# An inverse Fourier transform's last step: rows of four positions packed into three sets of matmul weights, with shared partial products added in PSUM

## The chip, the core and the metric

The kernel runs on one NeuronCore of one Trainium2 chip. The metric is the device time of one execution in microseconds (us); it was 1055.1 us (median of 3 runs, 1054.97 to 1055.27) before the change.

## The reference

Two batches of 3008 positions with 256 channels, all in float32, pass through a convolution by Fourier transform along the positions and then two feed-forward layers. Cut to what matters:

```python
X = np.fft.rfft(x, axis=1)                       # x: (2, 3008, 256)
Y = X * (filt_r + 1j * filt_i)[None]
y = np.fft.irfft(Y, n=3008, axis=1)
h = y.reshape(6016, 256) @ w_in                  # 256 -> 2048
g = np.where(h > 0, h, np.exp(np.minimum(h, 0)) - 1)
z = g @ w_out                                    # 2048 -> 256
h2 = z @ w2_in
out = (h2 * np.clip(h2 + 3, 0, 6) / 6) @ w2_out
```

## The kernel before, in words

The transform of length 3008 = 47 x 64 is done as two small transforms, each a matmul with a constant matrix: 47 points (`s1`, `s1t` forward, `i1` back) and 64 points (`s2` forward, `i2` back). The work is cut by batch b (0, 1) and by half h of the channels (128 channels each). The way back is: the product with the filter (`mult`, on DVE, with a sum on POOL), `i2_mm` on PE, `i2_evac` (a copy out of PSUM on ACT), a store to a scratch array in DRAM (`scr2`, 96 rows, line 233), a reload in another order (`v_load`, line 237), and `i1_mm`, the last step, whose results `i1_evac` copies into blocks of 512 positions (`yblk`). Those blocks are split into a high and a low part (`x_split`) for the matmuls of the feed-forward layers.

In `i1_mm` the reloaded data are the stationary operand (the weights, 96 rows by 128 channels for one of 32 places j) and the constant matrix `i1` (96 x 94) is streamed, so one j gives 94 positions. Five j share a PSUM bank and make a group, so a half has seven groups, the last one of two. The profile counts each float32 matmul of this kind as two PE records, and each has a weight load of its own.

Batch 0 is worked off ahead of the feed-forward layers, in an order written out by hand, the string `PROLOGUE`. A letter is a step, and the digits behind it are the half and the number: `S` the forward matmul and the filter, `I` the inverse of 64 points with its store, `V` the reload of a half, `O` or `o` one group of the last step (with its copy on ACT or on DVE), `X` the split of a block, `b` and `B` the first step of batch 1, `G` and `H` the first units of the feed-forward layer, `c` and `k` pieces of the preparation of weights, `F` the sign of a filter on POOL. So O00 is the first group of half 0, I15 the last inverse of half 1. Every engine works through its own instructions in the order in which the program issues them.

Batch 1 is put into the stream of the feed-forward units by slots (`pre` and `post`): a function `i1` places the reloads four slots ahead of a group, the group behind a unit, and the copy one slot later. Transfers of the rotated tiles go out on SP's queue in the program's order. Pools: `p4` has 21 tiles of 4 KB per partition, `p2` 20 of 2 KB, `ps` 7 banks of PSUM, `const` holds the matrices.

Of the kernel before, what the change touches and what calls it, by code (L numbers as in the profile page):

```python
# [9 lines left out]
F32 = mybir.dt.float32  # L10
# [9 lines left out]
NB, NA = 47, 64  # L20
NK2 = NB // 2 + 1
NJ = NA // 2
DFF = 2048
P = 128
NF = DFF // P
TJ = 2 * NB
TG = 5
KP = 96
# [19 lines left out]
def fft_conv_moe_moe2(ctx, tc, xp, fq, sg, cs1, cs1t, cs2, ci2, ci1, ident, w1i, w1o, w2i, w2o, out):  # L48
    nc = tc.nc
    const = ctx.enter_context(tc.tile_pool(name="const", bufs=1))  # L50
# [10 lines left out]
    def name(s):  # L61
        uid[0] += 1
        return f"{s}_{uid[0]}"

    def t4(shape, dt=F32):
        return p4.tile(shape, dt, tag="t4", name=name("t4"))

    def t2(shape, dt=F32):
        return p2.tile(shape, dt, tag="t2", name=name("t2"))

    def bank():
        return ps.tile([P, 512], F32, tag="ps", name=name("ps"))
# [4 lines left out]
    def evac(eng, dst, src):  # L77
        if eng is nc.scalar:
            nc.scalar.activation(dst, src, AF.Copy)
        else:  # L80
            eng.tensor_copy(dst, src)
# [10 lines left out]
    def flat(t):  # L92
        return t.rearrange("p k d -> p (k d)")
# [17 lines left out]
    mats = {}  # L111

    def load_mat(key, src, queue=nc.scalar):
        k, m = src.shape
        mats[key] = const.tile([k, m], F32, name=key)
        queue.dma_start(mats[key], src)
# [11 lines left out]
    scr2 = [[dram.tile([KP, NJ * P], F32, name=f"scr2_{b}_{h}") for h in range(2)] for b in range(B)]  # L128
# [5 lines left out]
    xin, filt, zs, ws, vin, accs, yblk = {}, {}, {}, {}, {}, {}, {}  # L134

    def x_load(b, h, q):
        xin[b, h, q] = t4([P, 8, P])
        nc.sync.dma_start(xin[b, h, q][:KP], xp[b, h, :, 8 * q : 8 * q + 8, :])
# [93 lines left out]
            nc.scalar.activation(flat(o), acc, AF.Copy)  # L232
        nc.sync.dma_start(by_a(scr2[b][h], g), o)

    def v_load(b, h, q):
        vin[b, h, q] = t4([KP, 8, P])
        nc.sync.dma_start(flat(vin[b, h, q]), scr2[b][h][:, 8 * q * P : 8 * (q + 1) * P])

    EDGES = [sum(BLOCKS[:i]) for i in range(len(BLOCKS) + 1)]
    JG = -(-NJ // TG)  # L240

    def i1_mm(b, h, jg):
        accs[h, jg] = bank()
        for j in range(jg * TG, min(NJ, jg * TG + TG)):
            nc.tensor.matmul(  # L245
                accs[h, jg][:, (j - jg * TG) * TJ : (j - jg * TG + 1) * TJ],
                vin[b, h, j // 8][:, j % 8, :], mats["i1"], start=True, stop=True,
            )

    def i1_evac(b, h, jg, eng):  # L250
        acc = accs.pop((h, jg))
        lo, hi = jg * TG * TJ, min(NJ, jg * TG + TG) * TJ
        for bl in range(len(BLOCKS)):
            a, e = max(lo, EDGES[bl]), min(hi, EDGES[bl + 1])
            if a < e:
                if (b, bl) not in yblk:
                    yblk[b, bl] = t4([P, 2, 512])
                evac(eng, yblk[b, bl][:, h, a - EDGES[bl] : e - EDGES[bl]], acc[:, a - lo : e - lo])
# [562 lines left out]
    pre = [[] for _ in range(NS)]  # L821
    post = [[] for _ in range(NU + 8)]

    def at(slots, n, fn, *args):
        slots[n].append(lambda: fn(*args))
# [12 lines left out]
    def fetch1(f):  # L838
# [12 lines left out]
        T00 T01 T02 S00 T03 F01 S01 T04 F01 S02 T05 F01 S03 I00 F01 S04 I01 F01 A10 A11 F01  # L851
        S05 I02 A12 A13 A14 I03 F01 A15 A16 I04 T10 c01 T11 c01 w00 I05 F01 x00 x01 V00 T12
        S10 T13 S11 T14 F01 S12 T15 S13 I10 F01 S14 I11 S15 I12 O00 I13 b00 c01 O01 I14 c01
        b01 o02 I15 M00 c01 b02 V10 c01 O03 X00 O04 w01 b03 c01 X01 k02 O05 O06 X02 k02 B00
        B01 B02 B03 G00 G01 k03 O10 o11 G02 X10 o12 X11 O13 X12 o14 k02 H00 H01 k02 O15 k01
        H02 O16
    """
    LOADS = [(0, None, q, None) for q in range(4)]
    for x in "F00 F01 F02 F03 X0 X1 X2 X3 F04 F05 F10 W0 M F11 F12 F13 F14 F15".split():
# [89 lines left out]
    for i, (l, p) in enumerate(ROUNDS):  # L949
        start = NU + 4 * GROUPS * (i - 1)  # L950
# [34 lines left out]
        at(pre, t + 4, i2_evac, 1, h, g)  # L985

    def i1(h, jg, t):
        for q in range(4):
            if (8 * q // TG) == jg:
                at(pre, t - 4, v_load, 1, h, q)  # L990
        at(post, t, i1_mm, 1, h, jg)
        at(pre, t + 1, i1_evac, 1, h, jg, nc.scalar)

    T = NI * NF
# [7 lines left out]
        mid(0, g, T + 12 + 2 * g)  # L1002
    for g in range(6):
        mid(1, g, T + 24 + 2 * g)
    for jg in range(7):
        i1(0, jg, T + 32 + jg)
    for jg in range(7):
        i1(1, jg, T + 42 + max(0, jg - 1))

    with tc.manual_schedule():  # L1010
        load_mat("s1t", cs1t, nc.sync)
        for key, src in (("id", ident), ("sg", sg), ("s2", cs2), ("i2", ci2), ("i1", ci1)):
            load_mat(key, src)
        three = const.tile([P, 1], F32, name="three")
        nc.vector.memset(three, 3.0)
        engs = (nc.scalar, nc.vector)

        warm = const.tile([P, 512], F32, name="warm")
        nc.gpsimd.memset(warm, 0.0)
        acc = bank()  # L1020
        for n in WARM:
            nc.tensor.matmul(acc[:, :n], warm[:, :P], warm[:, :n], start=True, stop=True)
        for h, g, q, r in LOADS:
            if q is not None:
                x_load(0, h, q)
            elif g is not None:
                f_load(0, h, g)
            elif r is not None:
                w_raw(0, r)
            else:  # L1030
                load_mat("s1", cs1, nc.sync)
        for jg in range(JG):
            s1t(0, 0, jg, engs[jg % 2])
        lead = w_chain(0, WLEAD, lambda f: None)
        f_sign(0, 0, 0)
        f_sign(0, 0, 1)
        nsign = 2
        for step in PROLOGUE.split():
            what, h, g = step[:-2], int(step[-2]), int(step[-1])
            if what == "T":  # L1040
                tr(0, h, g, nc.scalar if g > 1 else engs[g])
            elif what == "S":
                s2_mm(0, h, g)
                mult(0, h, g)
            elif what == "A":
                s1t(0, h, g, engs[g % 2])
            elif what == "I":
                i2_mm(0, h, g)
                i2_evac(0, h, g)
            elif what == "V":  # L1050
                for q in range(4):
                    v_load(0, h, q)
            elif what == "O":
                i1_mm(0, h, g)
                i1_evac(0, h, g, nc.scalar)
            elif what == "o":
                i1_mm(0, h, g)
                i1_evac(0, h, g, nc.vector)
            elif what == "k":
                steps(conv, g)  # L1060
            elif what == "c":
                steps(lead, g)
            elif what == "X":
                x_split(0, g, h)
            elif what == "F":
                for _ in range(g):
                    f_sign(0, *divmod(nsign, 6))
                    nsign += 1
            elif what == "x":
                x_load(1, h, g)  # L1070
            elif what == "w":
                w_raw(0, WLEAD + g)
            elif what == "b":
                s1_split(h, g)
            elif what == "B":
                s1_mm(1, h, g, parts.pop(("x", h, g)))
                s1_evac(1, h, g)
            elif what == "G":
                g1_half(units[g], 0)
            elif what == "H":  # L1080
                g1(units[g])
                if g:
                    g_split(units[g - 1])
            elif what == "M":
                split_mat("s1")

        for n, u in enumerate(units):
            place[0] = n
            for fn in pre[n]:
                fn()  # L1090
            if n >= NI:
                g1(u)
                g_split(units[n - 1])
            if n >= SKEW:
                g2(units[n - SKEW])
            for fn in post[n]:
                fn()
# [113 lines left out]
```

## Time and profile before

| What | Value |
|---|---|
| median of 3 runs | 1055.1 us |
| profiled execution, its own time | 1063.18 us |
| its span, first to last instruction | 1061.4 us |
| PE busy | 1048.8 us, 99% |
| DVE, ACT, POOL busy | 886.1, 797.7, 202.7 us |
| line 245 on PE (`i1_mm`) | 256 records |

The span is the profiled execution's first to last instruction; 1.8 us of its time lie around it. The profiled execution is 8.1 us longer than the median of the runs, so its durations make a sum against 1063.2 us, and the difference is carried over to the median. PE is TensorE's matmuls and PEld its weight loads, which the profile counts apart. DVE, ACT, POOL and SP are the vector, scalar, GpSimd and sync engines. [...]

### The profile page before, as it was taken

How to read it: one execution, taken by the hardware profiler on the slowest of the kernel's cores; microseconds unless marked ns; L12 is line 12 of the kernel's file. 1: busy time of each engine (PE TensorE's matmuls, PEld its weight loads, DVE VectorE, ACT ScalarE, POOL GpSimd, SP SyncE). 2: the span in 40 equal slices, each digit the busy share in tenths (PEclk: the TensorE clock that was granted, in tenths of full speed). 3: DMA queues.
4: the chain of work that ended last, by engine and by line, in shares of the span. 5: the costliest groups of instructions: out<-in, count | busy, mean ns of one | idle time of the engine just before them, and what ended most of it. 6: DMA issues, size and time to landing. Idle time of an engine off the chain costs nothing.

```text
span 1061.4 us, 14383 instructions
## 1 busy us (share of the span) xinstructions
PE 1048.8 (99%) x5022; PEld 918.7 (87%) x5022; DVE 886.1 (83%) x1427; ACT 797.7 (75%) x1437; POOL 202.7 (19%) x218
## 2 busy tenths in 40 slices
PE   9999999999999999999999999999999999999998
PEld 7688888888889989988888888888888888888998
DVE  2899999898886799889989978888888888888776
ACT  2478888897767888877877867777777777777766
POOL 1720000444546745300021100010010010000000
PEclk9999999999999999999999999999999999999999
DMA  9785100374645454610365710100100100100100
GB/s 278 246 263 198 50 16 1 106 222 151 196 135 178 153 193 152 213 55 6 133 236 161 231 73 21 60 1 21 60 14 27 40 18 18 41 1 1 40 1 35
DMA packets 57944, 107.31 MB, mean 101 GB/s; under 512 B 5008, under 2 KB 33680, under 8 KB 57872
## 3 DMA queue, kind: packets, MB, share of 16 engines
q1 hardware_dynamic: 52144, 88.21, 25.3%
q0 software_dynamic: 4896, 17.83, 5.4%
q8 instruction: 39, 0.64, 0.3%
q10 hardware_dynamic: 832, 0.36, 0.1%
q14 instruction: 33, 0.27, 0.1%
HBM read 69.42 MB, written 36.96 MB: 100 GB/s over the span
## 4 chain that ended last, share of the span: by engine, by line
PE 82%; ACT 7%; DVE 7%; issue 2%; DMA 2%; POOL 1%; SPq 0%; DVEq 0%; ACTq 0%; POOLq 0%
PE ps L90 24%; PE ps L88 24%; PE ps L89 24%; PE ps L158 2%; PE lone L88 1%; PE lone L90 1%; PE lone L89 1%; PE ps L245 1%; DVE t L85 1%; ACT t L84 1%; DMA scr<-t 1%; POOL t L217 1%; DVE t L679 1%; PE ps L202 1%; DVE t L634 1%
## 5 line engine op out<-in xcount | busy, mean ns | idle before, releaser
L88 PE MATMUL ps<-t,w 128*128 128x512 f32 (+1 forms) x1120 | 421.2, 376 | 2.3 <-DVE t L634 1.3
L90 PE MATMUL ps<-t,w 128*128 128x512 f32 (+1 forms) x1120 | 420.2, 375 | 0.7 <-DVE t L85 0.6
L89 PE MATMUL ps<-t,w 128*128 128x512 f32 (+1 forms) x1120 | 419.6, 375 | 0.2 <-DVE w L316 0.2
L88 PEld LDWEIGHTS ps<-t,w 128*128 128x128 f32 x1120 | 211.7, 189 | 29.4 <-DVE t L498 1.9
L90 PEld LDWEIGHTS ps<-t,w 128*128 128x128 f32 x1120 | 211.6, 189 | 28.4 <-DVE t L679 2.2
L89 PEld LDWEIGHTS ps<-t,w 128*128 128x128 f32 x1120 | 211.7, 189 | 25.9 <-DVE w L316 1.6
L679 DVE TENSOR_TENSOR t<-t,t 128x512 fp32r<-128x512 f32 (+1 forms) x256 | 175.7, 701 | 24.1 <-ACT t L674 22.5
L674 ACT ACTIVATE t<-t 128x512 fp32r<-128x512 f32 (+1 forms) x256 | 154.0, 616 | 6.1 <-DVE t L664 5.7
L628 ACT ACTIVATE t<-ps 128x512 f32<-128x512 f32 (+1 forms) x176 | 103.2, 586 | 64.9 <-PE ps L90 63.3
L634 DVE TENSOR_TENSOR t<-ps,t 128x512 f32<-128x512 f32 (+1 forms) x176 | 118.1, 679 | 14.2 <-ACT t L628 13.0
L664 DVE SCALAR_TENSOR_TENSOR t<-t,t 128x512 f32<-128x512 f32 (+1 forms) x144 | 97.6, 705 | 33.3 <-ACT t L648 32.7
L648 ACT ACTIVATE t<-t,three 128x512 f32<-128x512 f32 (+1 forms) x144 | 97.2, 707 | 37.3 <-DVE t L634 36.6
L495 ACT ACTIVATE t<-ps 128x512 f32<-128x512 f32 (+1 forms) x128 | 74.1, 579 | 30.1 <-PE ps L90 28.1
L84 ACT ACTIVATE t<-t 128x512 fp32r<-128x512 f32 (+2 forms) x108 | 66.2, 618 | 22.5 <-POOL t L217 20.0
L496 ACT ACTIVATE t<-t 128x512 f32<-128x512 f32 (+1 forms) x128 | 79.3, 619 | 4.1
L85 DVE TENSOR_TENSOR t<-t,t 128x512 fp32r<-128x512 f32 (+2 forms) x96 | 73.3, 769 | 10.6 <-ACT t L84 10.4
L548 POOL TENSOR_TENSOR t<-t,t 128x512 f32<-128x512 f32 (+1 forms) x12 | 16.2, 1351 | 286.0 <-DVE t L634 257.0
L498 DVE SCALAR_TENSOR_TENSOR ps<-t,ps 128x512 f32<-128x512 f32 (+1 forms) x76 | 50.4, 663 | 23.0 <-ACT t L496 22.5
L88 PE MATMUL ps<-t,t 128*128 128x512 f32 (+1 forms) x160 | 60.2, 376 | 0.6 <-DVE t L634 0.6
L89 PE MATMUL ps<-t,t 128*128 128x512 f32 (+1 forms) x160 | 60.1, 376 | 0.0
L90 PE MATMUL ps<-t,t 128*128 128x512 f32 (+1 forms) x160 | 60.1, 376 | 0.0
L85 DVE TENSOR_TENSOR t<-ps,t 128x512 fp32r<-128x512 f32 (+1 forms) x76 | 49.9, 656 | 0.1
(115 smaller groups left out, 1520.6 us busy)
## 6 DMA issues: line engine op xcount, KB each, us to landing
t<-in_fq SPq DMA_DIRECT2D x24, 512.0 KB, 6.2
scrw<-t SPq DMA_DIRECT2D x16, 512.0 KB, 2.8
w<-scrw POOLq DMA_DIRECT2D x16, 512.0 KB, 5.0
t<-in_xp SPq DMA_DIRECT2D x16, 384.0 KB, 6.0
scr<-t SPq DMA_DIRECT2D x24, 256.0 KB, 3.0
t<-scr SPq DMA_DIRECT2D x16, 384.0 KB, 5.2
scrx<-t SPq DMA_DIRECT2D x10, 512.0 KB, 3.3
t<-scr POOLq DMA_DIRECT2D x10, 512.0 KB, 6.1
```

Source lines behind the costliest of these rows:

```text
L84: nc.scalar.activation(hi, src, AF.Copy)
L85: eng.tensor_tensor(out=lo, in0=src, in1=_f32(hi), op=ALU.subtract)
L88: nc.tensor.matmul(acc, wh, xh, start=start, stop=False, skip_group_check=more)
L89: nc.tensor.matmul(acc, wl, xh, start=False, stop=False, skip_group_check=more)
L90: nc.tensor.matmul(acc, wh, xl, start=False, stop=stop, skip_group_check=more)
L496: nc.scalar.activation(t[:, :n], t[:, :n], AF.Exp, scale=-1.0)
L628: nc.scalar.activation(like(t, self.n), got(bank_, self.n), AF.Copy)
L634: nc.vector.tensor_tensor(out=like(self.h[key], n), in0=got(bank_, n), in1=like(u, n), op=ALU.add)
L648: nc.scalar.activation(like(r, n), h, AF.Relu, bias=three)
L664: stt(out=r, in0=r, scalar=6.0, in1=h, op0=ALU.min, op1=ALU.mult)
L674: nc.scalar.activation(gh[:, : self.n], g[:, : self.n], AF.Copy)
L679: nc.vector.tensor_tensor(out=gl[:, :n], in0=g[:, :n], in1=_f32(gh[:, :n]), op=ALU.subtract)
```

## The change

Of the 96 rows of a place j, the last step now needs three kinds of weights for four places. Rows of an even place fill partitions 0 to 95 of a tile, and 32 rows of the odd place beside it fill partitions 96 to 127 (tiles 0 and 1, eight such pairs each). The 64 rows that are left of two odd places fill a third tile, shared by all groups of the half. A group is four places (376 positions): two matmuls of 141 columns, which give the even place and one part of the odd one, and one matmul of 2 x 94 columns with weights from the shared tile, which adds the rest of both odd places in PSUM. A half has eight groups of three matmuls instead of seven with 32 in all. The matrix `i1` becomes two padded ones (`i1a`, 141 columns, `i1b`, 188), zeroed and loaded in six pieces on POOL's queue at the start. The reload of a half becomes eight transfers into three tiles instead of four into four, in runs of 512 bytes. `PROLOGUE` gets O07 and O17, and X12 moves behind o14. In batch 1 all eight transfers of a half go out four slots ahead of its first group. The warm-up's tile moves from `const` to `p2`.

```diff
-    def v_load(b, h, q):
-        vin[b, h, q] = t4([KP, 8, P])
-        nc.sync.dma_start(flat(vin[b, h, q]), scr2[b][h][:, 8 * q * P : 8 * (q + 1) * P])
+    def v_load(b, h):
+        by_j = scr2[b][h].rearrange("r (j d) -> r j d", d=P)
+        for i in range(2):
+            t = vin[b, h, i] = t4([P, 8, P])
+            nc.sync.dma_start(t[:KP], by_j[:, 16 * i : 16 * i + 16 : 2])
+            nc.sync.dma_start(t[KP:], by_j[0:64:2, 16 * i + 1 : 16 * i + 16 : 2])
+        t = vin[b, h, 2] = t4([P, 8, P])
+        for i in range(2):
+            nc.sync.dma_start(t[64 * i : 64 * i + 16], by_j[64:KP:2, 2 * i + 1 : NJ : 4])
+            nc.sync.dma_start(t[64 * i + 16 : 64 * i + 64], by_j[1:KP:2, 2 * i + 1 : NJ : 4])
+
+    def load_i1():
+        for key, n in (("i1a", TJ + NB), ("i1b", 2 * TJ)):
+            mats[key] = const.tile([P, n], F32, name=key)
+            nc.gpsimd.memset(mats[key], 0.0)
+        one, both = mats["i1a"], mats["i1b"]
+        nc.gpsimd.dma_start(one[:KP, :TJ], ci1)
+        nc.gpsimd.dma_start(one[KP:, TJ:], ci1[0:64:2, :NB])
+        for i in range(2):
+            r, c = 64 * i, TJ * i
+            nc.gpsimd.dma_start(both[r : r + 16, c : c + NB], ci1[64:KP:2, :NB])
+            nc.gpsimd.dma_start(both[r + 16 : r + 64, c + NB : c + TJ], ci1[1:KP:2, NB:])
...
     def i1_mm(b, h, jg):
-        accs[h, jg] = bank()
-        for j in range(jg * TG, min(NJ, jg * TG + TG)):
+        acc = accs[h, jg] = bank()
+        for i in range(2):
+            n = 2 * jg + i
             nc.tensor.matmul(
-                accs[h, jg][:, (j - jg * TG) * TJ : (j - jg * TG + 1) * TJ],
-                vin[b, h, j // 8][:, j % 8, :], mats["i1"], start=True, stop=True,
+                acc[:, 2 * TJ * i : 2 * TJ * i + TJ + NB], vin[b, h, n // 8][:, n % 8, :], mats["i1a"],
+                start=i == 0, stop=False, skip_group_check=True,
             )
+        nc.tensor.matmul(
+            acc[:, : IG * TJ].rearrange("p (a b) -> p a b", a=2)[:, :, TJ:], vin[b, h, 2][:, jg, :],
+            mats["i1b"].rearrange("p (a b) -> p a b", a=2), start=False, stop=True, skip_group_check=True,
+        )
...
     def i1(h, jg, t):
-        for q in range(4):
-            if (8 * q // TG) == jg:
-                at(pre, t - 4, v_load, 1, h, q)
+        if jg == 0:
+            at(pre, t - 4, v_load, 1, h)
...
-    for jg in range(7):
-        i1(1, jg, T + 42 + max(0, jg - 1))
+    for jg in range(8):
+        i1(1, jg, T + 42 + min(5, max(0, jg - 1)))
```

What this does to the engines' own orders shows at three places. The first is PE in batch 0, from the inverse I11 (its matmul is the first row) to the last inverse I15. Line 202 is the forward matmul of 64 points, line 222 the inverse, line 245 the last step; `t_97` and `t_98` are the first two reloaded tiles, `i_117` is `i1`. Before:

```order
L222 MATMUL ps_531<-t_118_484,i_115 128x512
L245 MATMUL ps_536<-i_117,t_97_429 128x94 x5
L222 MATMUL ps_544<-t_124_500,i_115 128x512
L245 MATMUL ps_554<-i_117,t_97_429 128x94 x3
L245 MATMUL ps_554<-i_117,t_98_431 128x94 x2
L222 MATMUL ps_563<-t_130_515,i_115 128x512
L245 MATMUL ps_573<-i_117,t_98_431 128x94 x5
L222 MATMUL ps_582<-t_136_529,i_115 128x512
L245 MATMUL ps_607<-i_117,t_98_431 128x94
```

After the change the last step is lines 266 and 270; `t_98`, `t_99` are the tiles of pairs, and `t_100` is the shared one:

```order
L222 MATMUL ps_542<-t_118_495,i_115 128x512
L266 MATMUL ps_547<-i1a,t_98_437 128x141 x2
L270 MATMUL ps_547<-i1b,t_100_443 128x2x94
L222 MATMUL ps_553<-t_124_511,i_115 128x512
L266 MATMUL ps_563<-i1a,t_98_437 128x141 x2
L270 MATMUL ps_563<-i1b,t_100_443 128x2x94
L222 MATMUL ps_570<-t_130_526,i_115 128x512
L266 MATMUL ps_580<-i1a,t_98_437 128x141 x2
L270 MATMUL ps_580<-i1b,t_100_443 128x2x94
L222 MATMUL ps_587<-t_136_540,i_115 128x512
```

Between two inverses a group of five matmuls has become one of two and one, and the first group reads the shared tile already.

The second place is SP's queue, from the last store of half 1 of batch 0 over the reload of that half to the raw weights behind it. Before:

```order
L233 DMA scr_0_1_83<-t_148_565 128x4x128
L233 DMA scr_0_1_83<-t_154_584 128x4x128
L237 DMA t_157_596<-scr_0_1_83 96x1024
L237 DMA t_158_598<-scr_0_1_83 96x1024
L237 DMA t_159_600<-scr_0_1_83 96x1024
L237 DMA t_160_602<-scr_0_1_83 96x1024
L267 DMA raw_629<-in_w1i 128x2x256
```

After the change:

```order
L233 DMA scr_0_1_83<-t_148_572 128x4x128
L233 DMA scr_0_1_83<-t_154_589 128x4x128
L239 DMA t_157_601<-scr_0_1_83 96x8x128
L240 DMA t_157_601<-scr_0_1_83 32x8x128
L239 DMA t_158_604<-scr_0_1_83 96x8x128
L240 DMA t_158_604<-scr_0_1_83 32x8x128
L243 DMA t_159_607<-scr_0_1_83 16x8x128
L244 DMA t_159_607<-scr_0_1_83 48x8x128
L243 DMA t_159_607<-scr_0_1_83 16x8x128
L244 DMA t_159_607<-scr_0_1_83 48x8x128
L292 DMA raw_631<-in_w1i 128x2x256
```

The four transfers of 96 rows have become eight of 96, 32, 16 and 48 rows at the same place between the last store and the raw weights, and those of the shared tile come last.

The third place is PE where half 1 of batch 0 begins its last step, behind a unit's three matmuls (lines 88 to 90, weights `w`). `t_157` and `t_158` are reloaded tiles. Before:

```order
L88 MATMUL ps_697<-t_171_637,w_604 128x512
L89 MATMUL ps_697<-t_171_637,w_604 128x512
L90 MATMUL ps_697<-t_172_638,w_604 128x512
L245 MATMUL ps_706<-i_117,t_157_596 128x94 x5
L245 MATMUL ps_713<-i_117,t_157_596 128x94 x3
L245 MATMUL ps_713<-i_117,t_158_598 128x94 x2
L88 MATMUL ps_721<-t_180_663,w_604 128x512
L89 MATMUL ps_721<-t_180_663,w_604 128x512
```

After the change, where `t_157` holds pairs and `t_159` is the shared tile:

```order
L88 MATMUL ps_705<-t_169_639,w_612 128x512
L89 MATMUL ps_705<-t_169_639,w_612 128x512
L90 MATMUL ps_705<-t_170_640,w_612 128x512
L266 MATMUL ps_714<-i1a,t_157_601 128x141 x2
L270 MATMUL ps_714<-i1b,t_159_607 128x2x94
L266 MATMUL ps_719<-i1a,t_157_601 128x141 x2
L270 MATMUL ps_719<-i1b,t_159_607 128x2x94
L88 MATMUL ps_725<-t_179_666,w_612 128x512
```

The place of the groups in PE's order is the same; the first one again reads the tile that is reloaded last.

## Rows read from the trace of the kernel before

**Rows 1.** The page, parts 1 and 4: busy us (share) xinstructions, and the chain.
```profile
PE 1048.8 (99%) x5022; PEld 918.7 (87%) x5022; DVE 886.1 (83%) x1427; ACT 797.7 (75%) x1437; POOL 202.7 (19%) x218
...
PE 82%; ACT 7%; DVE 7%; issue 2%; DMA 2%; POOL 1%; SPq 0%; DVEq 0%; ACTq 0%; POOLq 0%
```

**Rows 2.** Line 245 by shape: xcount, busy us, mean ns, idle before.
```profile
L245 PE MATMUL ps<-i,t 96*128 96x94 f32 x256 | 31.6, 273 | 0.0
```

**Rows 3.** Timeline of the weight loads: start us, us, engine, line, xcount.
```profile
54.39 1.09 PEld L245 LDWEIGHTS ps<-i,t 96*128 96x128 f32 x9 [0.24 <-issue]
```

**Rows 4.** Timeline of PE, 44 to 62 us, columns as above.
```profile
44.38 1.02 PE L202 MATMUL ps<-t,s 128*128 128x512 f32 x2
...
45.24 0.60 PE L171 MATMUL ps<-id,zt 128*128 128x128 f32 x4
...
54.39 1.25 PE L245 MATMUL ps<-i,t 96*128 96x94 f32 x10
...
60.27 1.13 PE L222 MATMUL ps<-t,i 128*128 128x512 f32 x2 [0.42 <-POOL t L217]
```

**Rows 5.** Line 237's first two sets of reloads: issues, then us to landing.
```profile
L237 SPq DMA_DIRECT2D t<-scr x4: 311/370/377, 48.3 to 49.7; - x4
...
DMA to landing us min/median/max: 5.5/7.1/8.2
...
L237 SPq DMA_DIRECT2D t<-scr x4: 321/370/411, 64.5 to 65.8; - x4
...
DMA to landing us min/median/max: 3.9/5.5/7.0
```

**Rows 6.** Timeline of PE, 64 to 79 us.
```profile
64.95 0.44 PE L88 MATMUL ps<-t,s_h 96*96 96x512 f32 x1
...
68.89 2.37 PE L245 MATMUL ps<-i,t 96*128 96x94 f32 x20
...
75.04 0.46 PE L88 MATMUL ps<-t,w 128*128 128x512 f32 x1
...
78.55 0.46 PE L88 MATMUL ps<-t,w 128*128 128x512 f32 x1
```

**Rows 7.** Windows: busy us of each engine, granted clock, DMA share, GB/s.
```profile
57.50:59.50 2.00, 1.99 (x13) 1.39 (x12) 1.99 (x4) 1.49 (x5) 0.96 (x2) 1.00 1.13 340
...
67.00:71.00 4.00, 4.00 (x30) 3.70 (x28) 3.83 (x8) 3.68 (x8) 0.00 (x0) 1.00 1.03 262
```

**Rows 8.** Timeline of PE at 87 us.
```profile
87.53 0.48 PE L88 MATMUL ps<-t,w 128*128 128x512 f32 x1 [0.76 <-DVE t L498]
```

**Rows 9.** Timeline of PE, batch 1.
```profile
305.36 1.35 PE L245 MATMUL ps<-i,t 96*128 96x94 f32 x10
...
314.31 1.25 PE L245 MATMUL ps<-i,t 96*128 96x94 f32 x10
...
315.35 0.44 PE L88 MATMUL ps<-t,w 128*128 128x448 f32 x1
...
339.71 2.37 PE L245 MATMUL ps<-i,t 96*128 96x94 f32 x20
```

**Rows 10.** Timeline of SP's issues, batch 1.
```profile
292.24 0.43 SPq L237 DMA_DIRECT2D t<-scr  x1
...
330.02 0.79 SPq L237 DMA_DIRECT2D t<-scr  x2
```

**Rows 11.** Window over both halves of batch 1.
```profile
304.00:360.00 56.00, 55.23 (x336) 52.94 (x335) 38.74 (x61) 43.05 (x95) 32.31 (x39) 1.00 0.44 139
```

**Rows 12.** POOL: its DMA issues by line, and its first product's wait.
```profile
L457 POOL DMA_DIRECT2D w<-scrw x16 | 8.6, 541 | 66.2 <-PE ps L90 66.2
...
12.86 1.04 POOL L147 TENSOR_TENSOR t<-t,sg 128x512 f32<-128x512 f32 x1 [11.59 <-DMA t<-in_fq]
```

**Rows 13.** Timeline of PE: line 158's first passes and later ones.
```profile
6.49 13.94 PE L158 MATMUL ps<-s1t,t 96*128 96x96 f32 x64 [0.53 <-DMA t<-in_xp]
...
35.49 3.49 PE L158 MATMUL ps<-s1t,t 96*128 96x96 f32 x30
```

More of the change, by code (lines that the diff above doesn't have):

```diff
@@ L239, in fft_conv_moe_moe2 @@
     EDGES = [sum(BLOCKS[:i]) for i in range(len(BLOCKS) + 1)]
     JG = -(-NJ // TG)
+    IG = 4
     def i1_mm(b, h, jg):
-        accs[h, jg] = bank()
-        for j in range(jg * TG, min(NJ, jg * TG + TG)):
+        acc = accs[h, jg] = bank()
+        for i in range(2):
+            n = 2 * jg + i
             nc.tensor.matmul(
-                accs[h, jg][:, (j - jg * TG) * TJ : (j - jg * TG + 1) * TJ],
-                vin[b, h, j // 8][:, j % 8, :], mats["i1"], start=True, stop=True,
-            )
+                acc[:, 2 * TJ * i : 2 * TJ * i + TJ + NB], vin[b, h, n // 8][:, n % 8, :], mats["i1a"],
+                start=i == 0, stop=False, skip_group_check=True,
+            )
+        nc.tensor.matmul(
+            acc[:, : IG * TJ].rearrange("p (a b) -> p a b", a=2)[:, :, TJ:], vin[b, h, 2][:, jg, :],
+            mats["i1b"].rearrange("p (a b) -> p a b", a=2), start=False, stop=True, skip_group_check=True,
+        )
@@ L250, in i1_evac @@
     def i1_evac(b, h, jg, eng):
         acc = accs.pop((h, jg))
-        lo, hi = jg * TG * TJ, min(NJ, jg * TG + TG) * TJ
+        lo, hi = jg * IG * TJ, (jg + 1) * IG * TJ
         for bl in range(len(BLOCKS)):
@@ L853, in fft_conv_moe_moe2 @@
         S10 T13 S11 T14 F01 S12 T15 S13 I10 F01 S14 I11 S15 I12 O00 I13 b00 c01 O01 I14 c01
-        b01 o02 I15 M00 c01 b02 V10 c01 O03 X00 O04 w01 b03 c01 X01 k02 O05 O06 X02 k02 B00
-        B01 B02 B03 G00 G01 k03 O10 o11 G02 X10 o12 X11 O13 X12 o14 k02 H00 H01 k02 O15 k01
-        H02 O16
+        b01 o02 I15 M00 c01 b02 V10 c01 O03 X00 O04 w01 b03 c01 X01 k02 O05 O06 X02 k02 O07 B00
+        B01 B02 B03 G00 G01 k03 O10 o11 G02 X10 o12 X11 O13 o14 X12 k02 H00 H01 k02 O15 k01
+        H02 O16 O17
     """
@@ L1004, in fft_conv_moe_moe2 @@
         mid(1, g, T + 24 + 2 * g)
-    for jg in range(7):
+    for jg in range(8):
         i1(0, jg, T + 32 + jg)
-    for jg in range(7):
-        i1(1, jg, T + 42 + max(0, jg - 1))
+    for jg in range(8):
+        i1(1, jg, T + 42 + min(5, max(0, jg - 1)))
     with tc.manual_schedule():
         load_mat("s1t", cs1t, nc.sync)
-        for key, src in (("id", ident), ("sg", sg), ("s2", cs2), ("i2", ci2), ("i1", ci1)):
+        for key, src in (("id", ident), ("sg", sg), ("s2", cs2), ("i2", ci2)):
             load_mat(key, src)
@@ L1016, in fft_conv_moe_moe2 @@
         engs = (nc.scalar, nc.vector)
-        warm = const.tile([P, 512], F32, name="warm")
+        warm = t2([P, 512])
         nc.gpsimd.memset(warm, 0.0)
+        load_i1()
         acc = bank()
@@ L1050, in fft_conv_moe_moe2 @@
             elif what == "V":
-                for q in range(4):
-                    v_load(0, h, q)
+                v_load(0, h)
             elif what == "O":
```

## The prediction, made before the changed kernel ran

> **What bounds the kernel now.** I read the page first: PE is busy 99% of the span and holds 82% of the chain that ended last [rows 1]. So work taken off PE pays where PE is fed, and a wait put on PE costs. Then the groups by shape: line 245 is 256 PE records for 128 matmuls [rows 2], two passes each, and each pass has a weight load of its own. The timelines say what a pass costs. Nine weight loads of one group start within 1.09 - 0.19 = 0.90 us, so 0.112 us apart [rows 3]. In a matmul of 512 float32 columns two passes take 45.24 - 44.38 = 0.86 us, 0.84 ns a column [rows 4]; 94 columns stream in 0.079 us. A pass of line 245 is thus set by its weight load. Last I read where the inverse step meets its reloads, because the change alters what the first group waits for. In the first half (b = 0, h = 0) SP issues four reloads from 48.34 us; the fastest lands 5.5 us, the slowest 8.2 us after issue, so between 53.8 and 57.9 [rows 5]. PE starts group O00 at 54.39 [rows 4]: it waits for the first of four only. In the second half they are issued from 64.50, land between 68.4 and 72.8 (3.9 and 7.0 after issue), and O10 starts at 68.89 [rows 5, 6]. So both halves work while three reloads are still in the air.
>
> **The change, part by part.**
>
> *PE passes.* Before, a half is 32 matmuls of two passes: 64 x 0.112 = 7.17 us, a group of five 1.12. After, it is 16 matmuls of 141 columns and 8 of 188. Both stream longer (0.118 and 0.158 us a pass) than a weight load takes, and in the 512-column rows a pass costs its columns and nothing else. A half is 32 x 0.118 + 16 x 0.158 = 6.30 us, a group 0.79. That saves 0.87 us a half. The other bound adds the 0.033 us that line 245 has beyond its columns to each pass: 7.9 us, 0.7 lost. I take the first, since it is the larger of two things that overlap in the rows.
>
> *Reloads.* The bytes stay: 96 x 32 x 512 B = 1.57 MB a half. Packets become 512 B instead of 4 KB, pieces have 96, 32, 16 and 48 rows, and all three tiles are needed by the first group, for its third matmul reads the shared tile that comes last. The cost is the landing of the last piece instead of the first. How long the eight move data, T, no row shows. From below: 512-byte stores run at 340 GB/s [rows 7], so 4.6 us. From above: the 96-row reloads run at 262 GB/s [rows 7], 1.5 us each; if the rate goes with the rows that a piece fills, each of the eight takes 1.5 us, 12 us when none overlap, 9 when half do, 6 when neighbours pair up (96 + 32, 16 + 48). The nearest row is the four reloads with the same bytes, 6.0 us. I take T = 6.5, the paired value and a half for imperfect pairs, and keep 4.6 and 9.
>
> [...]
>
> *First half.* The four landings spread over 57.9 - 53.8 = 4.1 us, 1.4 apart, so other transfers hold the queue until about 53.8 - 1.5 = 52.3. The last piece lands at 52.3 + 6.5 = 58.8. O00's third matmul starts then and ends at 59.1. Behind it on PE, in order, are I13 (0.86), O01 (0.79), I14, O02 and I15: I15 ends at 59.1 + 3 x 0.86 + 2 x 0.79 = 63.3. Before, I15 started at 60.27 [rows 4] and ended at 61.1, held by POOL's product (its wait in the same row). So I15 is 2.1 late, and with it the last store of the second half and its reloads.
>
> *Second half.* First issue 64.5 + 2.1 = 66.6. Before, the last landing came 8.3 after the first issue, 6.0 of it data; now 8.8, at 75.4. PE meanwhile does five groups (3.95) and the 3.94 us between 64.95 and 68.89 [rows 6], and is at O10 at 71.2: it waits 4.2 us. O10 ends at 75.7, before at 68.89 + 1.12 = 70.0: 5.7 late. The five full groups after it give back 5 x 0.33; O16, now full, and the new O17 cost 0.34 + 0.79. At 78.55, where the long weight-and-unit stream starts, PE is 5.2 late. At 87.53 PE ends a wait of 0.76 us for DVE [rows 8], which takes that much of the 5.2. DVE's work there hangs on H00, which starts at 75.04 [rows 6] and now 5.7 - 4 x 0.33 = 4.4 later. Both arrive together: **+4.4 us at 87.5**, and from there PE is fed.
>
> *Batch 1.* The groups lie in the fed stream: in one, line 88 follows 1.04 us after line 245 begins, with nothing waiting ahead [rows 9]. So 2 x 0.87 = 1.7 us is saved in full, if the reloads are in time. For h = 0 the first is issued at 292.24, and PE wants it at 305.36 [rows 9, 10]. For h = 1 the first goes at 330.02, the last lands 8.8 later, at 338.8; PE wants them at 339.71 - 0.87 = 338.8 [rows 9, 10]. No wait, but no room either: above T = 6.5 each us is lost here too. Raw weights now queue behind these pieces; they are for the next layer.
>
> *The rest, at nothing.* POOL's two memsets and six issues: an issue is 0.54, and a memset of a third of a tile I put at no more, so 4.3 us in all, under the 11.59 us in which POOL waits for the first filter [rows 12]. Without that cover it is 4.3 on the first product. ACT makes one copy more per half: it is busy 43 of 56 us around batch 1 with 95 operations [rows 11], so PE hides it; uncovered, four at that row's mean of 0.45 are 1.8.
>
> *Sum.* +4.4 - 1.7 = +2.7 us on the profiled 1063.2, which is 8.1 above the median of the runs. On the median: 1055.1 + 2.7 = **1057.8 us**. In the first part each us of T counts twice, since the second reload starts only after the first has let I15 through.
>
> **The rivals.**
>
> *The reloads arrive in time (not slower).* With T = 4.6 the first half lands at 56.9, I15 is 0.2 late, O10 1.9, and the front costs 0.6; with -1.7 the kernel runs in 1054.0. The turn is at T = 5.15, where the front costs as much as batch 1 gains. For it: 512-byte packets at 340 GB/s, and full-width pairs. Against: the 96-row loads are slow already. Within 0.2% of now up to T = 6.2. Chance 0.35.
>
> *The pieces hardly overlap.* At T = 9 the front costs 9.4, and batch 1's h = 1 waits 2.5: 1055.1 + 9.4 - 1.7 + 2.5 = 1065.3. [...] Chance 0.17.
>
> *The clock falls in the new waits.* [...] Chance 0.08.
>
> *Passes cost their columns and the gap.* 4 x 0.7 more instead of 4 x 0.87 less: about +3 over the forecast, 1061. Against: the 512-column rows. Chance 0.05.
>
> **How the numbers follow.** The forecast (T from 5.5 to 8, waits at O00 and O10) has 0.35. A measurement of this kernel can tell some 0.2%, 2.1 us, from no change. Slower by more needs T above 6.2 or a rival beyond: 0.35 x 0.8 + 0.17 + 0.08 + 0.05, near 0.55, as some of the first rival's doubt goes the same way; within: 0.36; faster, which needs T below 4.6 or DVE waits farther on that PE's delay fills, 0.09. The range: from 1053.4 (T at its lower bound and a front that costs nothing, 1055.1 - 1.7) to 1065.5 (T at 9, and the clock's fall), which leaves out T above 9, mixes of rivals and gains beyond the passes, some 0.15.
>
> **What would show it.** Line 266 and 270 passes about 0.118 and 0.158 apart. Line 270's weight load idle before O00 and O10 for some 4 us each, until a DMA of lines 243 and 244. Line 239 to 244 landings up to 9 us after issue. I15 two us later, 87.53 at about 92. In batch 1, no wait at h = 0 and a short or no wait at h = 1. I am wrong if the eight pieces move data in under 5 us, if PE's order lets other work past the waiting matmul, or if DVE catches up.

## The result, and the profile after

The changed kernel runs in 1068.3 us (median of 4 runs, 1067.6 to 1068.7), the kernel before in 1055.2 (4 runs): a ratio of 1.0124, with a 95% interval of 1.0112 to 1.0136. It is 13.1 us slower; 1057.8 was forecast, and the range ended at 1065.5.

The page of the changed kernel, parts 1 and 4, answers to [rows 1]:

```profile
PE 1042.9 (98%) x4958; PEld 910.9 (85%) x4958; DVE 884.4 (83%) x1427; ACT 797.3 (75%) x1441; POOL 205.2 (19%) x226
...
PE 80%; ACT 7%; DVE 6%; DMA 4%; issue 2%; SPq 1%; POOL 0%; DVEq 0%; ACTq 0%; POOLq 0%
```

PE's busy time is 5.9 us less (1048.8 to 1042.9), and yet the span is longer. Both this and DMA's share of the chain, 4% in place of 2%, say little: the first 64 passes of line 158 took 13.94 us in the first trace of before [rows 13] and 7.8 in its second, below, in which PE is busy for 1041.4 us, less than in the changed kernel, and DMA's share is 4% too. What has changed is seen in PE's timeline of the changed kernel (start, duration, count, and in brackets the idle time ahead and who ended it), which answers to [rows 4, 6, 8, 9]; PE now waits for the reloads:

```profile
45.16 1.12 PE L222 MATMUL ps<-t,i 128*128 128x512 f32 x2 [0.25 <-POOL t L217]
46.64 0.72 PE L266 MATMUL ps<-i1a,t 128*128 128x141 f32 x4 [0.36 <-DMA t<-scr]
51.30 0.96 PE L270 MATMUL ps<-i1b,t 128*128 128x188 f32 x2 [3.94 <-DMA t<-scr]
52.05 1.91 PE L222 MATMUL ps<-t,i 128*128 128x512 f32 x2
...
57.50 1.02 PE L222 MATMUL ps<-t,i 128*128 128x512 f32 x2
58.35 0.64 PE L266 MATMUL ps<-i1a,t 128*128 128x141 f32 x4
...
59.15 0.64 PE L266 MATMUL ps<-i1a,t 128*128 128x141 f32 x4
...
62.22 0.51 PE L88 MATMUL ps<-t,s_h 96*96 96x512 f32 x1
...
67.63 0.72 PE L266 MATMUL ps<-i1a,t 128*128 128x141 f32 x4 [1.24 <-DMA t<-scr]
73.05 0.97 PE L270 MATMUL ps<-i1b,t 128*128 128x188 f32 x2 [4.70 <-DMA t<-scr]
...
76.66 0.73 PE L266 MATMUL ps<-i1a,t 128*128 128x141 f32 x4
...
92.69 0.48 PE L88 MATMUL ps<-t,w 128*128 128x512 f32 x1 [0.75 <-DVE t L523]
...
318.66 0.48 PE L88 MATMUL ps<-t,s_h 128*128 128x512 f32 x1 [0.33 <-DVE t L215]
...
323.12 0.46 PE L88 MATMUL lone<-t,w 128*128 128x448 f32 x1 [1.05 <-ACT t L548]
```

Matmul records overlap (the inverse at 57.50 lasts 1.02 us, and the group behind it starts at 58.35), so what a matmul costs is read from one start to the next. The third matmul of O00 and that of O10 wait for the shared tile, 3.94 and 4.70 us, and their first matmuls 0.36 and 1.24. Behind each wait the same shapes take twice their time for a while: two records of an inverse 1.91 us at 52.05, and 1.02 at 57.50. Windows of the changed kernel (busy us of each engine, then the granted clock, DMA share, GB/s, as in [rows 7]) say why: 0.56 and 0.50 of the full clock, while PE was busy throughout. The third window, from the start, is for comparison in the last section:

```profile
51.30:57.00 5.70, 5.70 (x15) 3.91 (x16) 1.72 (x3) 2.24 (x6) 0.31 (x1) 0.56 0.31 96
...
73.00:76.60 3.60, 3.55 (x11) 3.37 (x12) 0.61 (x2) 1.06 (x2) 0.00 (x0) 0.50 1.05 395
...
6.00:13.40 7.40, 7.34 (x64) 7.17 (x64) 2.43 (x3) 3.01 (x4) 1.03 (x1) 1.00 1.05 314
```

### The profile page after: what moved, and what is told of

It is laid out like the page before. It is cut to its first block, busy times and chain, and to the rows that moved or that the text cites. A ratio compares the mean times of both kernels' runs of the same rounds, so it can differ in the third digit from the quotient of the medians.

```text
span 1065.8 us, 14306 instructions
## 1 busy us (share of the span) xinstructions
PE 1042.9 (98%) x4958; PEld 910.9 (85%) x4958; DVE 884.4 (83%) x1427; ACT 797.3 (75%) x1441; POOL 205.2 (19%) x226
## 4 chain that ended last, share of the span: by engine, by line
PE 80%; ACT 7%; DVE 6%; DMA 4%; issue 2%; SPq 1%; POOL 0%; DVEq 0%; ACTq 0%; POOLq 0%
PE ps L90 24%; PE ps L88 24%; PE ps L89 24%; DMA t<-scr 2%; PE lone L88 1%; PE lone L89 1%; PE lone L90 1%; PE ps L158 1%; DMA raw<-in_w1o 1%; DMA scr<-t 1%; ACT t L84 1%; DVE t L85 1%; PE ps L222 1%; ACT t L520 1%; PE ps L266 1%
## 5 line engine op out<-in xcount | busy, mean ns | idle before, releaser
L659 DVE TENSOR_TENSOR t<-ps,t 128x512 f32<-128x512 f32 (+1 forms) x176 | 117.8, 677 | 14.1 <-ACT t L653 12.8
```

Of the source, the lines that this page charges most:

```text
L659: nc.vector.tensor_tensor(out=like(self.h[key], n), in0=got(bank_, n), in1=like(u, n), op=ALU.add)
```

## The experiments

Times are medians; the kernel before ran beside each at 1055.0 to 1055.5. Ratios are of means, with a 95% interval, so one long execution moves a ratio and not the time.

**A second profile of before.** The trace that the prediction read was of an execution 8.1 us above the median.

> The kernel before, profiled once more. Theory 1: the 8.1 us by which its profiled execution was above the median lay in the first 24 us, where passes ran at the lower clock level; another execution starts its units near 57.2 us, as the run with batch 0 of before did, and not at 64.95, with the later trace unchanged. Theory 2: they lay elsewhere, and the units begin near 65 again.

It ran in 1055.8 us. PE's timeline of this execution:

```profile
5.75 1.97 PE L158 MATMUL ps<-s1t,t 96*128 96x96 f32 x16
7.96 5.85 PE L158 MATMUL ps<-s1t,t 96*128 96x96 f32 x48 [0.25 <-DMA t<-in_xp]
...
46.01 1.13 PE L222 MATMUL ps<-t,i 128*128 128x512 f32 x2 [0.24 <-POOL t L217]
47.30 1.32 PE L245 MATMUL ps<-i,t 96*128 96x94 f32 x10 [0.17 <-DMA t<-scr]
...
52.85 1.13 PE L222 MATMUL ps<-t,i 128*128 128x512 f32 x2 [0.27 <-POOL t L217]
53.81 3.93 PE L245 MATMUL ps<-i,t 96*128 96x94 f32 x34
57.52 0.44 PE L88 MATMUL ps<-t,s_h 96*96 96x512 f32 x1
...
61.47 2.37 PE L245 MATMUL ps<-i,t 96*128 96x94 f32 x20
...
80.13 0.48 PE L88 MATMUL ps<-t,w 128*128 128x512 f32 x1 [0.77 <-DVE t L498]
```

The 64 passes that took 13.94 us [rows 13] take 7.8 here, and the twelve records of transposes behind them 1.50 us and not 2.82. That makes up the 7.4 us between the two spans (1061.4 and 1054.0), so carrying the difference over to the median was right. This trace is the measure of the changed kernel from here on: at the wait for DVE that both have, 80.13 has become 92.69, 12.6 us late; the spans are 1054.0 and 1065.8, 11.8 apart (the medians 13.1). So batch 0 costs 12.6 in these two executions, and batch 1 gives back 0.8.

**Only batch 1 changed.** Batch 0 has the old matmuls, reloads and order; the main lines are shown.

```diff
     def i1_mm(b, h, jg):
         acc = accs[h, jg] = bank()
+        if b == 0:
+            for j in range(jg * TG, min(NJ, jg * TG + TG)):
+                nc.tensor.matmul(
+                    acc[:, (j - jg * TG) * TJ : (j - jg * TG + 1) * TJ],
+                    vin[b, h, j // 8][:, j % 8, :], mats["i1"], start=True, stop=True,
+                )
+            return
...
             elif what == "V":
-                v_load(0, h)
+                for q in range(4):
+                    v_load_old(0, h, q)
```

> Batch 0 as in the kernel before (32 matmuls a half, four reloads, the old order), batch 1 as in the changed one. Theory 1, all of the loss is batch 0's first groups: batch 1 alone gives what the traces show between units 1060 and 1250, 5.1 - 4.46 = 0.65 us, so 1054.5. Theory 2, the full 1.7 us of passes is saved once batch 0 is undisturbed: 1053.5. Theory 3, the new reloads or the two matrices cost elsewhere too: above 1056.

1054.5 us, ratio 0.9994 (0.9986 to 1.0003): the first theory's number. The whole loss is in batch 0. Batch 1's gain is smaller than a measurement can tell from nothing.

**PE kept busy through the waits.**

```diff
         acc = accs[h, jg] = bank()
+        if b == 0 and jg == 0:
+            for _ in range((18, 26)[h]):
+                nc.tensor.matmul(acc[:, :P], mats["id"], mats["s2"], start=True, stop=True)
```

> The changed kernel with 18 and 26 matmuls of 128 columns on matrices at rest, put ahead of groups O00 and O10, so that TensorE works through most of the two waits; their results are overwritten. Theory 1, the clock falls in the waits: work between 52.05 and 57.50 us in the changed kernel's trace is two inverses at 0.86 and two groups at 0.80, 3.3 us at the higher level, and it took 5.4; from 73.05 to 76.66 it is 1.8 at the higher level, and it took 3.6. So with TensorE kept busy about 4.0 us come back, 1064.3, and the granted clock stays near 1.0 through both stretches. Theory 2, only the late data cost: the time stays within 1 us of 1068.3, since the fillers end before the data come.

1065.3 us, 3.0 less than the changed kernel. Five of its six executions took 1064.9 to 1065.9 us, less than any of the changed kernel, and one 1075.9, which puts the ratio at 1.0113 (1.0085 to 1.0140), no lower than the changed kernel's; so the evidence is the trace. PE's timeline of this kernel, in which lines 269 and 273 are 266 and 270 of the changed one, and its window behind O00:

```profile
52.32 0.56 PE L273 MATMUL ps<-i1b,t 128*128 128x188 f32 x2 [1.61 <-DMA t<-scr]
52.71 1.02 PE L222 MATMUL ps<-t,i 128*128 128x512 f32 x2
...
56.02 1.02 PE L222 MATMUL ps<-t,i 128*128 128x512 f32 x2
...
72.03 0.56 PE L273 MATMUL ps<-i1b,t 128*128 128x188 f32 x2 [0.82 <-DMA t<-scr]
...
73.87 0.64 PE L269 MATMUL ps<-i1a,t 128*128 128x141 f32 x4
```

```profile
52.30:57.00 4.70, 4.68 (x21) 3.27 (x22) 2.06 (x4) 3.14 (x7) 0.00 (x0) 1.00 0.39 116
```

From O00's third matmul to I15 it is 56.02 - 52.32 = 3.70 us, and was 57.50 - 51.30 = 6.20; from O10's third to O12 73.87 - 72.03 = 1.84, and was 76.66 - 73.05 = 3.61. The granted clock stays at 1.00. So the lower clock costs 2.5 + 1.8 = 4.3 us in the changed kernel's trace, and useless matmuls ahead of a wait make the kernel faster; e9, below, shows the same well clear of the noise. It gave back 3.0 and not 4, as in this execution the reloads of half 0 went out 0.9 us later (41.57 and not 40.68) and their last piece landed 1.0 later.

**The shared tile second.**

```diff
-        for i in range(2):
+        def pair(i):
...
+        pair(0)
         t = vin[b, h, 2] = t4([P, 8, P])
         for i in range(2):
             nc.sync.dma_start(t[64 * i : 64 * i + 16], by_j[64:KP:2, 2 * i + 1 : NJ : 4])
             nc.sync.dma_start(t[64 * i + 16 : 64 * i + 64], by_j[1:KP:2, 2 * i + 1 : NJ : 4])
+        pair(1)
```

> The changed kernel with the order of the eight pieces changed: first pair tile, shared tile, second pair tile, so that O00 and O10 need six pieces and not eight. Theory 1, the wait is for the last of the pieces that a group needs, and they land in the order of issue: the second pair's share, 48.88 - 46.50 = 2.4 us in the first half and 70.21 - 67.50 = 2.7 in the second, comes off each wait, 5.1 in all, and up to 4 more if the clock then falls less: 1059 to 1063.2. Theory 2, all eight move side by side and end together whatever the order: 1068.3.

1063.3 us, ratio 1.0079 (1.0067 to 1.0091), the slow end of the first theory. The two waits of the third matmuls fell from 8.6 to 4.4 us together. In the changed kernel's trace the eight pieces land in the order of issue, from 46.1 to 51.2 us in half 0 and from 67.0 to 72.9 in half 1, and the two groups' third matmuls start at 51.30 and 73.05, behind the last. The clock still fell in e2, to 0.63 and 0.52 behind its two waits.

**The inverses ahead of the groups.**

```diff
-        ... I12 O00 I13 b00 c01 O01 I14 c01
-        b01 o02 I15 M00 c01 b02 V10 c01 O03 ...
+        ... I12 I13 b00 c01 I14 c01
+        b01 I15 V10 O00 O01 o02 M00 c01 b02 c01 O03 ...
```

> The changed kernel with the inverses I13, I14 and I15 and the second half's reload V10 issued ahead of O00, O01 and o02. Theory 1, the wait of O00 also holds up I15, with it the second half's last store and its reload: I15 then runs near 52.5 us on the changed kernel's clock, about 5 earlier, O00 behind it finds its data, V10 goes out near 57 and not 62.4, the units begin near 59.5 and not 62.2, and O10 waits some 3.5 us and not 5.9: 5.3 us off, up to 4 more from the clock, 1059 to 1063. Theory 2, the inverses are held by the products on DVE and POOL anyway, so TensorE waits for them as long: within 1 us of 1068.3.

1062.2 us, ratio 1.0072 (1.0059 to 1.0085). O00's wait is gone, the second reload goes out at 56.18 and not 62.44, and O10 still waits 2.8 us:

```profile
56.18 0.32 SPq L239 DMA_DIRECT2D t<-scr  x1
...
66.55 0.56 PE L270 MATMUL ps<-i1b,t 128*128 128x188 f32 x2 [2.83 <-DMA t<-scr]
```

The wait of half 0 had been passed on to half 1 through I15, its store and its reload.

**Nothing changed but which landing is waited for.** Neither bytes nor matmuls differ from the kernel before:

```diff
-                for q in range(4):
+                for q in (3, 2, 1, 0):
                     v_load(0, h, q)
```

> The kernel before with batch 0's four reloads issued in reverse order, so that group O00 and O10 wait for the last landing instead of the first; no byte and no matmul changes. Theory 1, the loss of the change is the wait for the last landing: O00 begins 3.2 us later (the spread of the landings in an undisturbed front, 49.9 against 46.7), I15 2.5 later, and O10 near 68, 6.9 later; with the clock's fall another 2 to 4: 1062 to 1066. Theory 2, the loss comes from the pieces themselves (eight transfers, 512-byte runs): within 2 us of 1055.

1072.4 us, ratio 1.0177 (1.0157 to 1.0198): worse than the change, and 6 us over the first theory's upper end. PE's timeline of it, its window behind O10 (busy us, then the granted clock), and its second set of reloads (issues, then us to landing). This profiled execution was 6.3 us above the median; it lost them ahead of O00, as the last section shows:

```profile
57.26 2.42 PE L245 MATMUL ps<-i,t 96*128 96x94 f32 x10 [3.31 <-DMA t<-scr]
...
63.98 1.25 PE L245 MATMUL ps<-i,t 96*128 96x94 f32 x10
...
77.89 4.55 PE L245 MATMUL ps<-i,t 96*128 96x94 f32 x20 [4.11 <-DMA t<-scr]
...
94.06 0.46 PE L88 MATMUL ps<-t,w 128*128 128x512 f32 x1
```

```profile
77.80:92.00 14.20, 14.11 (x58) 13.51 (x59) 4.97 (x11) 4.02 (x8) 0.00 (x0) 0.50 0.93 314
```

```profile
L237 SPq DMA_DIRECT2D t<-scr x4: 321/370/411, 69.3 to 70.6; - x4
...
DMA to landing us min/median/max: 4.0/5.7/7.1
```

The waits are 3.31 and 4.11 us, as long as expected. What exceeds the expectation is the clock: behind O10 it stays at half for over 14 us, with PE busy in nearly all of them.

**The same, with PE kept busy.** Fillers as above, 14 and 18, in the kernel with reversed reloads.

> The kernel before with the reloads in reverse order (as e7) and 14 and 18 matmuls of 128 columns ahead of O00 and O10, on matrices at rest, results overwritten; they are shorter than the waits. Theory 1, the clock's fall is the larger part of e7's loss: in its trace the work from 57.26 to 63.98 is 4.0 us at the higher level and took 6.7, that from 77.89 to 94.06 took 16.2 and in the kernel before 8.6 (61.47 to 70.04); 10.3 us come back, near 1062, the time of the waits alone. Theory 2, the waits and what hangs on them are the loss: within 3 us of 1072.

1063.4 us, ratio 1.0071 (1.0055 to 1.0087): 9.0 us back. PE's timeline, line 248 being 245:

```profile
51.47 1.35 PE L248 MATMUL ps<-i,t 96*128 96x94 f32 x10 [1.28 <-DMA t<-scr]
...
55.52 1.25 PE L248 MATMUL ps<-i,t 96*128 96x94 f32 x10
...
69.18 2.41 PE L248 MATMUL ps<-i,t 96*128 96x94 f32 x20
...
77.79 0.46 PE L88 MATMUL ps<-t,w 128*128 128x512 f32 x1
```

From O00 to o02 4.05 us in place of 6.72, from O10 to the unit behind O15 8.61 in place of 16.17: the clock is 10.2 of e7's 17 us, the waits and what they delay the rest.

**Runs of 512 bytes alone.** Each of batch 0's four reloads takes every fourth place; rows, order and matmuls as before.

```diff
         vin[b, h, q] = t4([KP, 8, P])
+        if b == 0:
+            by_j = scr2[b][h].rearrange("r (j d) -> r j d", d=P)
+            nc.sync.dma_start(vin[b, h, q], by_j[:, q:NJ:4])
+            return
...
-                vin[b, h, j // 8][:, j % 8, :], mats["i1"], start=True, stop=True,
+                vin[b, h, j // 8 if b else j % 4][:, j % 8 if b else j // 4, :], mats["i1"], start=True, stop=True,
```

> The kernel before with batch 0's four reloads in runs of 512 bytes (places j of one remainder by four in each tile), 96 rows each as before; the first group needs all four tiles. Matmuls unchanged. Theory 1, the rate hangs on the rows that a transfer fills and not on its runs: the four move their data in some 6 us as before, and the time is that of the reversed order, 1062 to 1066. Theory 2, runs of 512 bytes are slower: last landings over 9.5 us after the first issue, and a time above the reversed order by twice the difference. Theory 3, they are faster, as stores of 512 bytes were (340 GB/s): below it.

1072.2 us, ratio 1.0161 (1.0147 to 1.0174). The time is e7's, as the first theory had it, but the last landing comes 10.0 us after the first issue, as the second had it. Both times lie far above the number set for them, with the granted clock at 0.987 and 0.984 of full over the whole span; so the time alone doesn't price the runs. The reloads do. Line 239's second set here, and then line 244's in the changed kernel with SP's issues of the first and last piece:

```profile
L239 SPq DMA_DIRECT2D t<-scr x4: 571/588/1306, 63.3 to 65.3; - x4
...
DMA to landing us min/median/max: 4.6/6.4/8.0
```

```profile
L244 SPq DMA_DIRECT2D t<-scr x2: 412/444/475, 65.0 to 66.4; - x2
...
DMA to landing us min/median/max: 6.5/6.5/6.6
```

```profile
62.44 0.32 SPq L239 DMA_DIRECT2D t<-scr  x1
...
66.42 0.41 SPq L244 DMA_DIRECT2D t<-scr  x1
```

From first issue to last landing: 70.6 + 7.1 - 69.3 = 8.4 us with 4 KB runs, 65.3 + 8.0 - 63.3 = 10.0 with 512-byte runs, 66.4 + 6.5 - 62.4 = 10.5 with runs of 512 bytes in eight pieces. In half 0 it is 8.2, 9.7 and 10.5. So short runs cost about 1.5 us beside e7. The pieces' share, 0.5 to 0.8, isn't shown, as the same transfers differ by more from trace to trace: in batch 0 the eight pieces took 9.9 to 11.3 us, and the four transfers of before 8.2 to 9.5.

**Both remedies, and further.** e5 has the shared tile second and the inverses ahead; e8 puts two groups between the inverses and a unit ahead of O10; e10 is e5 with the shared tile's transfers cut by groups; e11 is e10 with e8's two groups.

```diff
-        ... I12 I13 b00 c01 I14 c01
-        b01 I15 V10 O00 O01 o02 M00 ...
+        ... I12 I13 b00 c01 I14 O00 c01
+        b01 I15 V10 O01 o02 M00 ...
...
-        ... I12 I13 b00 c01 I14 O00 c01
-        b01 I15 V10 O01 o02 M00 ...
+        ... I12 I13 b00 c01 O00 I14 O01 c01
+        b01 I15 V10 o02 M00 ...
...
+        def rest(c):
+            g, lo = slice(4 * c, 4 * c + 4), 16 * c + 1
+            for i in range(2):
+                js = slice(lo + 2 * i, 16 * c + 16, 4)
+                nc.sync.dma_start(t2_[64 * i : 64 * i + 16, g], by_j[64:KP:2, js])
+                nc.sync.dma_start(t2_[64 * i + 16 : 64 * i + 64, g], by_j[1:KP:2, js])
+
+        pair(0)
+        t2_ = vin[b, h, 2] = t4([P, 8, P])
+        rest(0)
+        pair(1)
+        rest(1)
```

The first part is `PROLOGUE` of e5 against e4, the second that of e8 and e11 against e5 and e10 (e8 also moves G02 from behind o11 to ahead of O10), and the last part is e10's transfers of the shared tile (`t2_`), for c = 0 ahead of the second pair tile and for c = 1 behind it.

> The changed kernel with the shared tile loaded second, the inverses ahead of the groups, and O00 between I14 and I15. Theory 1, waits for pieces and the clock's fall behind them are all of the loss: I15 stays near 51.8, the units begin near 58.3, O10's shared tile lands near 64.2 where TensorE wants it at 62.8, so a wait of 1.4 is left and little of the clock's fall: 1058 to 1060. Theory 2, the two remedies take away the same time: no better than 1062.2, the better of the two alone.

1057.5 us, ratio 1.0027 (1.0016 to 1.0038), better than expected: the longest wait left between I12 and the groups of half 1 is 1.09 us, and the granted clock stays at 1.00.

> As e5, with O00 between I13 and I14, O01 between I14 and I15, and the unit G02 (0.65 us) ahead of O10. Theory 1, what is left of the loss in e5 is TensorE idle before I14 and I15 (1.09 and 0.72 us) and at O10 (1.07): a group of 0.80 goes into the idle time, and G02 covers 0.65 of the wait; 1.4 less, 1056.0. Theory 2, those places are held by POOL's product and by the last landing, which move with the groups: 1057.5 as e5.

1057.6 us, ratio 1.0024 (1.0015 to 1.0033): the second theory's number. O00, moved forward, waited 2.40 us for its shared tile and held up I14, as in the changed kernel.

> As e5, with the shared tile's four pieces cut in two (places 0 to 15, then 16 to 31), the first four of them ahead of the second pair tile: O00 and O10 need 0.79 MB and not 1.05 of the half's 1.57. Theory 1, a group's wait goes with the bytes issued up to its last piece: in e5 the four shared pieces landed over 64.33 - 61.70 = 2.6 us, half of that comes off, and O10's wait of 1.07 is gone: 1056.4. Theory 2, smaller pieces take as long as larger ones (a cost for each transfer): 1057.5 or above, and more landings after 64.

1056.2 us, ratio 1.0009 (1.0000 to 1.0018): as the first theory had it. O10 waits no more, and twelve transfers had landed 9.6 us after the first was issued, not later than eight.

> As e10, with O00 between I13 and I14 and O01 between I14 and I15, as e8 had them. Theory 1, in e10 TensorE still idles 1.09 and 0.72 us before I14 and I15 while O00's data have landed at 49.4; O00 then ends near 49.8, I14 starts at most 0.1 late, one more group lies in idle time, and the units begin 0.8 earlier: 1055.4, the time before. Theory 2, O00's wait for its last piece holds I14 and I15 again, as in e8: 1056.2 or above.

1056.0 us, ratio 1.0002 (0.9988 to 1.0015): between the two theories, and not to be told from e10, as the ratio is lowered by one execution of the kernel before at 1063.3. More of the idle time is used, and O00 still waits 0.33. This puts the new step in both batches at the time of the old; no version was found that is clearly faster than the kernel before. The nearest is e3.

## Why the prediction was wrong

**Right: the place, and the wait as the cause.** The sign, O00 and O10 as the places, the shared tile as what is waited for, and the way from O00's wait over I15 to the second reload are as the prediction had them. O00 waits 3.94 + 0.36 = 4.3 us, 4.4 forecast. A group takes 59.15 - 58.35 = 0.80 us, 0.79 forecast, and batch 1 waits for no reload, as forecast. e3 shows that the loss lies in batch 0 alone, e7 that such a wait is enough for a loss with the old matmuls and bytes, e10 that the loss is all but gone where neither group waits, and e4 that half 0's wait is paid again in half 1.

**The step that failed: "The clock falls in the new waits", left out of the sum and given 0.08.** Waits of 4 us were in the forecast, and the higher clock was assumed behind them. The granted clock was 0.56 and 0.50 there, and by the rows beside e1 that is 4.3 us; fillers returned 3.0 of them. The range's upper end, 1065.5, names the clock's fall, but no row of before gives a price for it; the runs showed these 4.3 us, and the time ended above the range, for the other misses below. The trace of before had no wait of that length, its longest on PE is 1.3 us, so no row could show the fall, and that was no evidence against it: the clock was at 0.56 behind 3.94 us idle and at 0.50 behind 4.70, and at 0.50 behind 4.11 in e7.

**A term that was mis-sized: the last landing.** I had 8.8 us from first issue to last landing in half 1; it was 10.5. The reload also went out 0.9 us later behind I15's end than in before (62.44 - 58.35 = 4.1, and 57.02 - 53.81 = 3.2), 0.7 of it because the last store landed 3.0 us after its issue and not 2.3. So O10 waited 1.24 + 4.70 = 5.9 us and not 4.2. That O00's wait came out right is in part luck: for half 0 the prediction put other transfers ahead of the eight pieces and so had 10.5 us, and both halves took 10.5.

The prediction took the lower bound for the runs from stores of 512 bytes, 340 GB/s [rows 7], which these reloads don't reach (245 GB/s from 46.0 to 51.3 us in the changed kernel, 226 from 67.6 to 73.0): by the reloads beside e6 the runs' length is the larger part, about 1.5 us, and the pieces' few rows, on which the working was spent, the smaller: the 0.5 to 0.8 us left for them lie within the scatter of the traces, and twelve pieces (e10) took 9.6 us.

**A credit that wasn't there: 0.76 us at 87.53.** DVE's wait was to take that much of the delay. It is still 0.75 at 92.69: it lies between works that both moved, and absorbs nothing.

**A gain that was half lost: batch 1.** By the starts of the units behind them in the two traces, six groups of a half save 0.32 each and the last two cost 0.35 and 0.80 more, which is 0.77 a half, 1.5 in all, as forecast within 0.2. But 0.8 arrived. PE now waits 0.33 us for DVE's product at 318.66, where it had no wait, and 1.05 at 323.12 for ACT, 0.75 before: 0.6 of the gain went into waits for work whose time PE doesn't set. The two waits lie behind the first three groups of half 0. That the stretch was fed throughout was read from one group [rows 9].

**The sum once more**, from I12 to DVE's wait: 92.69 - 45.16 = 47.5 us, and 80.13 - 46.01 = 34.1 before, so 13.4 longer; that is 0.8 more than the 12.6 above, as I12 began that much earlier in this execution. Waits 4.3 + 5.9, less the 0.17 and 0.27 that before had there; the clock 4.3; passes -1.2 (a half was 3 x 1.09 + 3.71 = 7.0 and is 8 x 0.80 = 6.4): 12.9. Some 0.5 stays unexplained. The forecast's front was 4.4; of the 9.0 us between the two the clock's 4.3 is the largest part.

## What to carry to other kernels

When one matmul of a group needs the last of several transfers where before each needed its own, price the spread of the landings, once for each wait and again for each later transfer that this wait holds up; here the order of issue alone (5.0 us, e2) was worth more than the passes saved (1.2 to 1.5 us a batch). If a forecast contains a wait of several us on TensorE, put the clock into the sum as well, even if no row of the trace has such a wait: here waits of 3.94 and 4.70 us had 4.3 us of lower clock behind them. And here 0.6 of the 1.5 us gained on a busy engine ended at waits for work that it doesn't drive, so look for those behind every place that gets shorter.

## What the hardware showed that was not expected

The clock's return differs widely. With groups of 141 and 188 columns behind O10 it was back after 3.6 us; in e7, with passes of 94 columns that are set by their weight loads (0.112 us apart [rows 3], where the columns take 0.079), PE was busy for 14.1 of 14.2 us at 0.50. The first trace of before had the like at its start: 13.94 us for 64 passes of 96 columns [rows 13], where the second one took 7.8. Whether the kind of pass is the cause was not tried.

The idle time alone doesn't say whether the clock falls: in e8 it stayed at 1.00 behind a wait of 2.40 us, in e2 it was 0.63 behind 0.43 and 2.14, and in e7's profiled execution, ahead of O00, it fell behind a wait of only 1.70 us for a product on DVE, with 20 passes of line 158 in 3.62 us behind it, and 0.50 still from 35 to 40 us; this is where that execution lost its 6.3 us. These are the rows of e8, of e2 and of e7:

```profile
51.08 0.56 PE L273 MATMUL ps<-i1b,t 128*128 128x188 f32 x2 [2.40 <-DMA t<-scr]
...
51.10:55.00 3.90, 3.90 (x20) 2.94 (x21) 2.34 (x3) 2.75 (x7) 0.79 (x1) 1.00 1.14 318
```

```profile
50.40:55.00 4.60, 4.60 (x13) 3.03 (x14) 2.35 (x4) 2.14 (x5) 1.27 (x1) 0.63 1.00 263
```

```profile
31.03 3.62 PE L158 MATMUL ps<-s1t,t 96*128 96x96 f32 x20 [1.70 <-DVE t L215]
...
35.00:40.00 5.00, 5.00 (x17) 3.66 (x16) 0.97 (x1) 1.77 (x3) 2.61 (x3) 0.50 0.58 176
```

And the granted clock that a window shows can miss a slow stretch. The first trace of before has, in this window, half as many records as the changed kernel in the window of 6.00 to 13.40 shown above, in both at a granted 1.00:

```profile
6.00:13.40 7.40, 6.91 (x33) 6.94 (x33) 0.97 (x1) 1.18 (x2) 0.55 (x1) 1.00 1.03 305
```

This trace holds its first record of the granted clock at 23.82 us, where the shapes become fast, that of the changed kernel at 5.15; so the 1.00 of this window lies ahead of any record. At the start of this execution the time of a shape, 13.94 us for the 64 passes and not 7.8, says more than the window.
